# Sum of squares of the first three gate groups on TensorE instead of VectorE, in a gated recurrence followed by a PReLU MLP (one core)

## The chip, the core and the metric

The kernel runs on one core of a Trainium2 chip. The metric is the time of one execution on the device in microseconds (us), here a median over a few runs. The core's engines are TensorE (PE; its weight loads are PEld), VectorE (DVE), ScalarE (ACT), GpSimd (POOL) and SyncE (SP), which here issues all the DMAs. Each engine works through its own instructions in order and waits on semaphores for the others.

## The reference, cut to what matters

```python
# q, k, v, a_re, a_im: (4, 8, 768, 48) f32; w_in (384, 2048), w_out (2048, 384), alpha (2048)
mag = sqrt(a_re*a_re + a_im*a_im)
scale = minimum(mag, 0.999) / (mag + 1e-6)
ar, ai = a_re*scale, a_im*scale                  # complex gate per token and channel
for t in range(768):                             # state S: (4, 8, 48, 48), complex
    S = (ar[t] + i*ai[t])[..., None] * S + outer(k[t], v[t])
    y[t] = q[t] @ real(S)
x = y.transpose(0, 2, 1, 3).reshape(3072, 384)
h = x @ w_in
out = (maximum(h, 0) + alpha * minimum(h, 0)) @ w_out
```

## The kernel before

**Tiling.** The 768 tokens of each of the 4 batches are cut into 6 chunks of 128, so there are 24 *units* (batch, chunk). The gates are made in 9 *groups* (`GATES`): groups 0, 1 and 2 hold 1, 2 and 3 chunks of batch 0, the other six hold 3 chunks each. A group is a tile of 128 partitions by `N` values (3 rows of 128 channels times its tokens: `N` = 384, 768, 1152) in six planes `x, c, f, d, e, y`.

**Gates.** `gates(g, b, c0, c1)` loads `a_re` and `a_im` into `x` and `y` (L255), squares both on ScalarE into `c` and `d` (L265, L267; group 0, which is worked in two halves, L301, L303), adds them on VectorE (L269; group 0 L305), takes roots on ScalarE (L272 to L277; group 0 L310 to L314), corrects with VectorE products that read the sum again (L279 and L289; group 0 L316 and L323), writes unit complex numbers and decays, and then forms running products of the phases (`product`, L416 and L418). The phases of whole chunks leave by the products of L507, the sums of L510 and the DMAs of L512 to a DRAM tile `phs`; the decays leave by L401 to `decs`.

**Units.** `loads` brings each unit's queries and keys (`KQ`, L657, L659), phases (`PP`, L665, read back from `phs`; one buffer) and decays (`T`, L672, read back from `decs`). `unit(u)` rotates queries and keys by the phases (VectorE, L742 and L744, `WQ` and `KQ`), then climbs six levels: at each VectorE multiplies `KQ` by decays (L797, six per unit), ScalarE copies (L820, L836), and TensorE makes 32x32 products into `ps_lv` (`meet`, L759). After the sixth L797 come transposes (L868), state products (L880), level outputs (L900), states (L916 on ScalarE, L918 on VectorE) and L930, which ends `ps_y`. The rows go to DRAM (L949) and come back as `xT` (L962).

**MLP.** `features` (L978, into `ps_h`), PReLU in two steps (ScalarE L985, VectorE L987) and `outputs` (L997, into `ps_o`) for groups of one or two chunks; the last three groups use a form with fewer products (L1097, L1172). The weights come as 64-bit words and are turned to f32 by ScalarE (L588 to L592), GpSimd (L596) and VectorE (L598, L600).

**PSUM.** `ps_h` has two buffers, `ps_o` and `ps_y` one each (`ps_y` spans two banks).

**Order.** Every task is a generator that yields before each step. The string `ORDER` gives the sequence, and with it the order on every engine and in SP's queue of DMAs: one letter runs one step. A to I are the gate groups 0 to 8, J `loads`, K `half_rows`, L `loads_v`, M `pieces`, N and O the weights, P to Z and a to m units 0 to 23, n `loads_x`, o the MLP, p `mixes`, q `late_outputs`. The planning values that the yields carry (`ACT(N, t)` and the like) have no effect when the kernel is built.

Of the kernel before, what the change touches and what calls it, by code (L numbers as in the profile page):

```python
# [9 lines left out]
F32 = mybir.dt.float32  # L10
# [3 lines left out]
AF = mybir.ActivationFunctionType  # L14
ALU = mybir.AluOpType
PSUM = bass.MemoryType.PSUM
DRAM = bass.MemoryType.DRAM

P = 128
# [11 lines left out]
    "AAJMMAABAJAAAAAAAAAAAAAAAAAAAAMMMBJMAAAAAAAAAAKANAOAAAABAAANAAAKANNNABAMAJNBKOAKBOOKAABMAKABAAALOAAB"  # L31
    "LAKNOLNAALBOLANNAALBBLAAKBAKBBAKABABKMAAKBAAOAABAAAAAABABBABAAABAOOABABMANAAAAAAABAAAKBABNABBNBNOBOC"
    "BOCBJNNBLBOJBBOONBBNBBOCBBPBCBPPJLJMJCLKBNBCMBCJBPLBPCBOPPJCPBBBPOBPPBBNBPBBNNBBCPPMLPBLBBPLKBPKBCCC"
    "PLOKBKBPKBBBBCBPKCOOPKBPPPCPBPBCBPPPPBBPBCBBPBBPBBPBPCBPMPBCCBCBPNBKLCCNLCNPCPOCOJDCNDPPPJCOJNNCCCNJ"
    "OCNOOLCNOPCNKOMNNCPQPDJCQDLCDNQPPDQQQLCDQDKQQMCLNDQDOKPQQMODQLOOJQJDKQJDOLCQnOJOLDDJQNJOQLQLOOoLoDDC"
    "QLoQRQoLQQLQooooQQCoQDKNJooooRoMQoQCRCCoooooQoRDQQQCODDCONNCooRQRLoDCLRoMoLoCRRLCoooooCJoRDKCRKooooo"
    "RCDoRQLCDLCoooCoRKoOLCDJCQDCCoLDCRRDDCooooooLCQCooCLCoCoCoLCLCCCLCRCCLCKOCRCRLoCooCRRRCRRoRRCoCRCQQC"
    "CRCQCCoRKCRQRQQCQOORRoRCCQCCooRRCNQDoLoDLoNoDNoooNDoEDNNoEOJoDJRJDRLoooooDDoLDRRRLDRRLRDNDNEJDJSDDRo"
    "oJDESDEDSRDRJESSnJSoLESDoLoLODJSSJDSDLLTSDJoELoooooSSSDLoLooooJSSoDDDoSEDLoooSToSoJooJSSSDoSSDSSoooo"
    "ooSTSDETooooTToSEEoEDoooooSDToSEDTSESSSSDooLDTLoooLEEDSLToLSLoooooDLELoTJDSSSDoooooTTSDSESSSLoDooooo"  # L40
    "SEEDTLLoTKoooooDDDToTEJLDDDDoooooTEUJTDKoDoooKTToDoLoToooTLoUoDJoTLToooToEJoDonooToDEoDTKoUoDJooToUo"
    "EoEUTUEoETEDDDJTooUooDoUUoDooToToTTDoLoLoULoLDULLoooUUoDoLooooDoULoLoELooooLoUULoTLUTLJoooooFUEUoETT"
    "TUUUUTTTUooooTToUETUUFEoUEooooEoUVoUEoooooVVKJJUUEUUEUUoFooLEFLoUoLEUFJVUELoVJoUJooooVJEoFVEJEVoEUoo"
    "oUUUEVoEUoLoVVLEoooEoLEoVEJooooJVEWoFEnVVLoVELoLoooEoKVVEoELVEoJFooooJWoVoVFooWLooLVVEEWoLWVoLWVEFJV"
    "VVJEooVoVoooEKoWKoJEoooVEWWooVWoVoEFWVVVEVVEWELWEELooFEELoWLEoEoLoWWLVLoWEEEEVLLooooooLWEWLEoLEFELEK"
    "FFVVVooWooLooVVVVVFFFVLXKEoEWooooooEWWEEWWJoWWJoooWoEJWoWJoFJWoEWFFWWWWoEoELoLEoJoLoEoFXEooooFooooXo"
    "ooooKXWXLXFWoXoGGXLoXooooJWoLXoLWoFWXoXWFXWoFWXFWWoWXoXFFoFLoXoGFJFnGooooXXoJFoFLoLXXXXLGFLoooooXLFX"
    "XXoGoLFGFLoooooooFXoooGFoJoYJXoJFoJXFGKoooXFYFXoXFYJFooooGXXXYoYXLYFooLXFYFKoLoYoYLXXFZLFXLoXYXFLoXX"
    "XoooYXoFGLGFYYLoYGoFJoYFYJoooFoFZoLFoJoYJGKooooFJGYFYLooYYYLoJYYZGLLFoooooZLoFGYZYZoYZYKJFZZooooYFoZ"
    "YoYFGZYYFYFFYYFZFLFZFFLoYLoooZLooLoFFFFFYFZLFZYYYLFoZLYYFLYoooFZYLaZFLoFoooZZZZoYZZLZoGYFFLLoooZoZGo"  # L50
    "LGoFZJoZFFFGJoooooFooZFFZZFZZZGLoonoFLooLaoFoLoooaJoLoZoaJGoLZooaJaGoaoHoLZZLaaZoHGGoGZGZGGaZLGaLooo"
    "ooaZGaLoaJoZaZaooooGJoHaooHGoooaoaGLaHoooLoGLaaJaHoaJaaJoooooHoGbaoaGHoooaoGaobbJKHoaGaoaoaGaaHoLKoG"
    "JoboLGobLGoLGoooGbLoHGHbLboJbHoGJLaoLbbGLooooGoGHobLGaLaHbLGbabLaabaaGoLaooooLGbboGoGHbGooooJbGbGGKo"
    "bbboJobJbGGbcbbJobGGoooboGcbooooGbGoHbGbGcbbbLGcGLoooGbLcGHcGGJoboJcoLJGGGobLGccLGoobKcbLobHLbobbLoc"
    "obHoGHGdbLGHooooccocGoJoJHoooLcocdJooLconJHLoooocLcHoccccoccLGoJdcGGooocodHocHoHdHoHcGGGcoooGooocGGc"
    "GccccodGLLoooGcodooooLoddJoooLocdoLoIHIoHLdooooLHooLHdcoLdcoLdcLocJHcocddoHoHooKcoooILdocoLHoIHdcdLH"
    "LddoIKdooooJdoIddJoddKdHoHooodoHdoIoHedHHodeHIdddodoHLeHLoLoIHodLHoHLHeIHoLdLoooeeJHeHLoLdddHoooeeoH"
    "JHdedHLoJooooeIoLIeLeoeJddoLHoooLeeoLoHdIHeodJoHIHoooeeoJeeeeoeJeoeIJeoenJHIHoooeJIoeooHeHoHfeeoeHfe"
    "eoLLHoHHJHoHHeHoLfeoLILJHHHHofLooooofeLHfeHfLeHKoeIeLoKffLeHoooooefHeoeLgIIfogJLooooIoooffofoHJILooo"
    "ooHLffoJIoJfHHoooooKHofofJooLfffffofKoJgooHofgIoooggoIHIofofHIoIIoofoHKfooHofogfffoffggoLHLoLogoLoHI"  # L60
    "oLgoooILofnoIfgLgLgLfffoLggJoLgfKoooofooooIgLogfooLfIfofggggggogoohgogIhhLJJJIIhIooooogogoIIoogggggg"
    "oLILogoJIoJgIohJgIILgIgooohLIIgoJgIoIghILhIoIghILoLhhIooooIoIhIoJoLihILJooohhohLoLohLohoooLioJIIoLho"
    "LoJiJooohohooJhhiohhihJhihnoIIIhIoIIhIIIIooohIoIhIioIhihhhhhIihoLihLLLohhhLIIIIIiooooLohhiILiIoLiILo"
    "hLoooiiIoLohihohoLIoooILiIiLoLiiiiiioJioJioIIiIoooioiojoioIiiijIiiJooLojLoJoIoJoLjoooiLoIioLojIjiiiI"
    "jiiooooojjooooLojLiiJoooojLopoLjojiiLoooJjoLoojjJLojLLoooooJojLojooJjjjjjJojjJopjojookkkoojojooojjkj"
    "jojjokLkoLkLokJokoLokLoLoookLjooLjkJkokLLokkLoooLokooooLojjjLokjkjojkjjkojkkLlkookkopkJokJpoookokook"
    "oklkkkkLkLoookJlooLoLolooJokJopoJoLllJklnkLllokoooooklolokooollkkLLLolkoololoooJoLloJoLoooLlmlololoo"
    "oloLoLlooolLmooomololloolpmooolomlomopoomoomomoooomooomoollllllmmomoolomomoooolmoonoolllmmomlmomlmol"
    "lomomoooooooomLooLooooLoLoooLoooooooLoqLoooLooLomLooooLooLooLomLoooooooopooooomoooomoooooooooooooooo"
    "oooooooomomomoomoomomoooomomomoqlmqlmqmmmqqmqoooooqqoqoooooqoqqoqooqoqqooqoqqoqoqooqooqqoooooqoqqoqo"  # L70
    "ooooooooooqoooqoooqqoqqoqooooooooooqqooqoooooqqoqqoqooqoqooqoqqoqqqqqqqqoooooooooooqoqqoqoqooqooqooq"
    "oqoqooqoqoqoooqqqoqqonoooooooooooooooqooqqoqoqqoqqooooooooooooqqoqoqoooqooooooooooooqqqooqooqoooqoqq"
    "oqooooooooqqoooooooooqoooooooooooqooqoooqqoooqoqqqoqooooooooqoqoooqoqooooqqoqqoqooqoqooqqqoqoqqqqqqq"
    "ooooqoooooooqoqqoqooqqqoqoqooooooooooooqqqqqqoqqoooooooooooooooooqqqqoqqoqqooooooooooooooooooqoqqqoq"
    "oqoooooooooooooooooqqooooooooooooqoooqoqoooqoqqoqqoooooooooooqqqooooooqoqqoqqooqoqooqoqqqqqooooooooo"
# [29 lines left out]
def kernel(  # L105
# [32 lines left out]
    nc = tc.nc  # L138
    B, HP, _, D, S = q.shape
    H = 2 * HP  # L140
    DM, DF = w_in.shape
# [19 lines left out]
    ps = ctx.enter_context(tc.tile_pool(name="ps", bufs=1, space=PSUM))  # L161
# [6 lines left out]
    ident = consts.tile([P, P], F32, tag="ident")  # L168
# [22 lines left out]
    for h in (16, 32):  # L191
        by_row[h] = []
        for m in range(HC // h):
            t = next(column)
# [11 lines left out]
    DVE = ACT = POOL = PE = DMA = step  # L206
# [21 lines left out]

    def gates(g, b, c0, c1):
        C = c1 - c0  # L230
        n = C * P
# [26 lines left out]
        if g:  # L258
# [9 lines left out]
            t = yield DVE(N, t)  # L268
            TT(out=c, in0=c, in1=d, op=ALU.add)  # L269

            t = yield ACT(N, t)
            nc.scalar.activation(d, c, AF.Abs_reciprocal_sqrt)  # L272
# [6 lines left out]
            TT(out=e, in0=e, in1=c, op=ALU.mult)  # L279
# [9 lines left out]
            TT(out=c, in0=c, in1=d, op=ALU.mult)  # L289
            ts = yield ACT(N, ts)  # L290
            nc.scalar.activation(c, c, AF.Copy, scale=1.0 / (1.5 * GATE_SCALE))
        else:
            parts = [[z[:, N // 2 * h:N // 2 * (h + 1)] for z in (x, c, f, d, e, y)] for h in range(2)]
            ready, tf, ts, txs = [None, None], [None, None], [None, None], [None, None]

            def enter(h):
                x, c, f, d, e, y = parts[h]
                yield ACT(N // 2, tx)
                nc.scalar.activation(x, x, AF.Identity, scale=1.5, bias=bias_tiny)
                yield ACT(N // 2)  # L300
                nc.scalar.activation(c, x, AF.Square, scale=GATE_SCALE)  # L301
                r = yield ACT(N // 2, t)
                nc.scalar.activation(d, y, AF.Square, scale=1.5 * GATE_SCALE)  # L303
                ready[h] = yield DVE(N // 2, r)
                TT(out=c, in0=c, in1=d, op=ALU.add)  # L305

            def root(h):
                x, c, f, d, e, y = parts[h]
                r = yield ACT(N // 2, ready[h])
                nc.scalar.activation(d, c, AF.Abs_reciprocal_sqrt)  # L310
                r = yield ACT(N // 2)
                nc.scalar.activation(e, d, AF.Square)
                r = yield ACT(N // 2)
                nc.scalar.activation(f, e, AF.Abs_reciprocal_sqrt)  # L314
                yield DVE(N // 2, r)
                TT(out=e, in0=e, in1=c, op=ALU.mult)  # L316
                yield DVE(N // 2)
                STT(out=d, in0=e, scalar=3.0, in1=d, op0=ALU.subtract, op1=ALU.mult)
                for p, w in ((y, -0.75), (x, -0.5)):
                    txs[h] = yield DVE(N // 2)  # L320
                    STT(out=p, in0=p, scalar=w * GATE_SCALE, in1=d, op0=ALU.mult, op1=ALU.mult)
                ts[h] = yield DVE(N // 2)
                TT(out=c, in0=c, in1=d, op=ALU.mult)  # L323
# [937 lines left out]
```

## Time and profile before

| | |
|---|---|
| runs | 816.86, 817.37, 820.89 us; median 817.37 us |
| the profiled execution | 820.38 us, its span 818.6 us, mean granted TensorE clock 0.968 |
| busy, share of the span | TensorE 681.1 us (83%), VectorE 693.9 (85%), ScalarE 520.3 (64%), GpSimd 222.2 (27%) |
| chain that ended last | TensorE 65%, VectorE 14%, DMA 10%, ScalarE 4% |
| DMA | 129.20 MB on SP's queue, 59.3% of 16 engines' span |

The span runs from the first to the last instruction of the profiled execution; what lies around it makes 1.8 us of the execution's own time. A busy share is an average over stages with different limits, so the stretches below matter more than the shares. "L742" is line 742 of the kernel before.

### The profile page before, as it was taken

To read this page: it belongs to the slowest core of one execution; us is meant where nothing else is said; L and a number is where in the kernel's file an instruction comes from. 1 tells how busy PE (TensorE), PEld (TensorE's weight loads), DVE (VectorE), ACT (ScalarE), POOL (GpSimd) and SP (SyncE) were. 2 spreads that over 40 slices of the span, in tenths; PEclk is the share of its full clock that TensorE was granted. 3 is DMA by queue.
4 is the path that set the end of the run, shared out by engine and by line. 5 is a ranking of instruction groups with operands and counts; after the bars stand their busy time and mean duration, and the time that the engine had idled before them with its cause. 6 is when DMAs were issued, how large, how long until landed. Compare 5 with 4: busy or idle time off the path is not lost.

```text
span 818.6 us, 27870 instructions
## 1 busy us (share of the span) xinstructions
PE 681.1 (83%) x11680; PEld 539.0 (66%) x11680; DVE 693.9 (85%) x1191; ACT 520.3 (64%) x1307; POOL 222.2 (27%) x293
## 2 busy tenths in 40 slices
PE   0003128659998999999999999999999999999997
PEld 0003126537776777767777777777777777899997
DVE  5999999999989899999999989998787775456574
ACT  8777998669666777876876697555756544312121
POOL 7231343051604310531245054003200000233342
PEclk9999659979999999999999999999999999999999
DMA  8594895593689589738865867787566622101000
GB/s 242 176 294 128 266 296 158 177 253 101 182 235 197 140 194 272 174 90 279 195 168 141 253 160 180 223 197 184 117 182 134 153 77 56 44 1 40 1 21 20
DMA packets 186598, 130.99 MB, mean 160 GB/s; under 512 B 74728, under 2 KB 176872, under 8 KB 186088
## 3 DMA queue, kind: packets, MB, share of 16 engines
q1 hardware_dynamic: 186472, 129.20, 59.3%
q8 instruction: 92, 1.51, 0.8%
q14 instruction: 34, 0.28, 0.1%
HBM read 100.82 MB, written 35.71 MB: 167 GB/s over the span
## 4 chain that ended last, share of the span: by engine, by line
PE 65%; DVE 14%; DMA 10%; ACT 4%; SPq 2%; issue 2%; POOL 1%; DVEq 0%; ACTq 0%; POOLq 0%
PE ps_o L997 19%; PE ps_h L978 18%; PE ps_m L1172 7%; PE ps_lv L759 5%; PE ps_y L1097 4%; PE ps_h L1097 4%; PE ps_y L900 3%; DVE KQ L797 2%; PE ps_kv L880 2%; PE ps_y L930 2%; DMA VL<-in_v_dram 2%; DVE gate L507 2%; PE ps_kt L868 1%; DVE gate L416 1%; DMA T<-decs 1%
## 5 line engine op out<-in xcount | busy, mean ns | idle before, releaser
L978 PE MATMUL ps_h<-xT,w_in_sb 128*128 128x256 f32 (+1 forms) x960 | 227.0, 369 | 2.1 <-DVE w_in_sb L600 1.6
L997 PE MATMUL ps_o<-w_out_sb,g_sb 128*128 128x384 f32 x576 | 222.1, 501 | 4.8 <-DVE g_sb L987 4.7
L978 PEld LDWEIGHTS ps_h<-xT,w_in_sb 128*128 128x128 f32 x960 | 170.9, 195 | 51.3 <-DVE w_in_sb L600 2.2
L797 DVE TENSOR_TENSOR KQ<-KQ,T 96x1024 f32<-96x1024 f32 x120 | 148.4, 1237 | 25.8 <-PE ps_lv L759 19.2
L997 PEld LDWEIGHTS ps_o<-w_out_sb,g_sb 128*128 128x128 f32 x576 | 102.5, 191 | 44.9 <-DVE g_sb L987 6.5
L985 ACT ACTIVATE g_sb<-ps_h 128x256 f32<-128x256 f32 (+1 forms) x160 | 57.9, 362 | 73.0 <-PE ps_h L978 72.2
L759 PE MATMUL ps_lv<-WQ 96*32 96x32 f32 x2304 | 34.4, 203 | 83.6 <-DVE WQ L742 70.2
L759 PEld LDWEIGHTS ps_lv<-WQ 96*32 96x32 f32 x2304 | 26.3, 116 | 105.9 <-DVE WQ L742 71.0
L916 ACT ACTIVATE St<-St,T 96x48 f32<-96x48 f32 x352 | 84.0, 325 | 4.6 <-DVE St L918 4.3
L987 DVE SCALAR_TENSOR_TENSOR g_sb<-g_sb,al,ps_h 128x256 f32<-128x256 f32 (+1 forms) x160 | 71.3, 446 | 13.7 <-ACT g_sb L985 13.1
L1160 POOL TENSOR_TENSOR sums<-g_sb 128x128 f32<-128x128 f32 x48 | 21.8, 475 | 185.5 <-DMA VL<-in_v_dram 110.6
L416 POOL TENSOR_TENSOR gate<-gate 128x72 f32<-128x72 f32 x42 | 34.5, 822 | 133.7 <-ACT gate L446 130.9
L596 POOL TENSOR_SCALAR top<-top 128x768 f32<-128x768 f32 x16 | 44.1, 2755 | 74.6 <-ACT top L588 63.2
L820 ACT COPY WQ<-KQ 96x1024 f32<-96x1024 f32 x48 | 50.0, 1041 | 18.9 <-DVE KQ L797 18.3
L416 DVE TENSOR_TENSOR gate<-gate 128x576 f32<-128x576 f32 (+5 forms) x84 | 50.7, 604 | 1.1
L900 PE MATMUL ps_y<-A,VL 64*48 64x64 f32 x2304 | 41.9, 220 | 4.4 <-issue 4.3
L900 PEld LDWEIGHTS ps_y<-A,VL 64*48 64x48 f32 x2304 | 39.0, 122 | 6.8 <-issue 6.7
L507 DVE TENSOR_TENSOR gate<-gate 128x1152 f32<-128x1152 f32 (+2 forms) x36 | 42.8, 1220 | 0.8 <-POOL gate L492 0.7
L1135 ACT ACTIVATE rl<-g_sb 128x256 f32<-128x256 f32 x24 | 10.0, 416 | 50.0 <-DVE g_sb L1128 50.0
L773 ACT ACTIVATE A<-ps_lv,columns 128x64 f32<-128x64 f32 x144 | 37.4, 336 | 6.2 <-PE ps_lv L759 5.9
L836 ACT COPY W<-KQ 96x512 f32<-96x512 f32 x48 | 30.8, 641 | 16.2 <-DVE KQ L797 8.7
L759 PE MATMUL ps_lv<-KQ,W 96*32 96x32 f32 x1536 | 24.7, 204 | 18.5 <-ACT W L836 17.4
(168 smaller groups left out, 1355.7 us busy)
## 6 DMA issues: line engine op xcount, KB each, us to landing
T<-decs SPq DMA_DIRECT2D x48, 384.0 KB
PP<-phs SPq DMA_DIRECT2D x24, 387.0 KB
KQ<-in_q_dram SPq DMA_DIRECT2D x48, 192.0 KB
decs<-gate SPq DMA_DIRECT2D x7, 1152.0 KB
phs<-gate SPq DMA_DIRECT2D x14, 576.0 KB
KQ<-in_k_dram SPq DMA_DIRECT2D x40, 192.0 KB
vsc<-in_v_dram SPq DMA_DIRECT2D x48, 144.0 KB
VL<-vsc SPq DMA_DIRECT2D x48, 144.0 KB
```

The lines of the kernel that those rows point to most:

```text
L416: on(4 * k).tensor_tensor(out=m, in0=w[:, 1::-1].unsqueeze(2).to_broadcast([P, 2, 2, k]), in1=pairs_of(u), op=ALU.mult)
L507: TT(out=m[:, a], in0=U5[:, 1 + a], in1=turned(off3, o)[:, a].unsqueeze(1).unsqueeze(3).to_broadcast([P, L // 2, nb, 2]), op=ALU.mult)
L759: nc.tensor.matmul(t[64 * i + j:64 * i + j + HC // 2, p], lhsT=keys(n, g), rhs=queries(n, g), start=True, stop=True)
L797: nc.vector.tensor_tensor(out=x, in0=x if x0 is None else x0, in1=m, op=ALU.mult)
L900: nc.tensor.matmul(o, lhsT=Vp[h][64 * i:64 * i + 64, s, e_ * D:(e_ + 1) * D], rhs=a, start=False, stop=False)
L916: nc.scalar.activation(St[:, n], before[:, n], AF.Copy, scale=T[0:D2, n, TL - 4 + s:TL - 3 + s])
L978: nc.tensor.matmul(p, lhsT=w_in_sb[:, f // 2, kk, f % 2 * P:(f % 2 + 1) * P], rhs=x_of[m][:, kk], start=(kk == 0), stop=(kk == NK - 1))
L985: nc.scalar.activation(gt, p, AF.Relu, scale=-1.0)
L987: nc.vector.scalar_tensor_tensor(out=gt, in0=gt, scalar=al_1[:, f:f + 1], in1=p, op0=ALU.mult, op1=ALU.add)
L997: nc.tensor.matmul(sums[0], lhsT=gt[:, c * P:(c + 1) * P], rhs=w_out_sb[:, f], start=(f == 0), stop=(f == NF - 1))
L1097: nc.tensor.matmul(o, lhsT=lhs, rhs=rhs, start=(at in (0, 5)), stop=(at in (4, 8)))
L1172: nc.tensor.matmul(banks[k][:, half], lhsT=lhs, rhs=rhs, start=(j == 0 and half == 0), stop=(j == NF // 2 - 1 and at in (2, 3, 5, 6)))
```

## The change

In groups 0, 1 and 2 the addition of the two squares on VectorE (L269 and L305) is gone. TensorE multiplies each of the two planes by the identity and sums both products in PSUM: two matmuls for each bank. Group 0 takes a buffer of `ps_h` for each half (192 columns), group 1 the two banks of `ps_y` (384 columns each), group 2 both buffers of `ps_h` and `ps_o` (384 columns each). The steps that read the sum now read PSUM: one ScalarE root and two VectorE products for each piece. Group 2's piece is a bank, so each of these three steps becomes three instructions. Groups 3 to 8 are as before. The string `ORDER` is another one.

```diff
+SUMMED = 3
...
+    def bank_views(banks, n):
+        if banks == ["y"]:
+            z = ps.tile([P, 2, 512], F32, tag="y", name="ps_y")[:, :, 0:n // 2]
+            return [(z, lambda row: row.rearrange("p (z s) -> p z s", z=2))]
+        n //= len(banks)
+        return [(ps.tile([P, DM], F32, tag=tag, name="ps_" + tag, bufs=2 if tag == "h" else 1)[:, 0:n],
+                 lambda row, i=i: row[:, n * i:n * (i + 1)]) for i, tag in enumerate(banks)]
+
+    def sum_of_squares(z, a, b_):
+        for i in range(z.shape[1] if len(z.shape) > 2 else 1):
+            parts_ = [x[:, i] if len(z.shape) > 2 else x for x in (z, a, b_)]
+            for j in range(2):
+                nc.tensor.matmul(parts_[0], lhsT=ident, rhs=parts_[1 + j], start=j == 0, stop=j == 1)
...
-            t = yield DVE(N, t)
-            TT(out=c, in0=c, in1=d, op=ALU.add)
+            if g < SUMMED:
+                banks = {1: ["y"], 2: ["h", "h", "o"]}[g]
+                t = yield PE(4 * N * 1.68e-3, t, takes=[R[z] for z in banks])
+                sums_ = bank_views(banks, N)
+                for z, row in sums_:
+                    sum_of_squares(z, row(c), row(d))
+            else:
+                t = yield DVE(N, t)
+                TT(out=c, in0=c, in1=d, op=ALU.add)
+                sums_ = [(c, lambda row: row)]
...
-            nc.scalar.activation(d, c, AF.Abs_reciprocal_sqrt)
+            for z, row in sums_:
+                nc.scalar.activation(row(d), z, AF.Abs_reciprocal_sqrt)
...
-            TT(out=e, in0=e, in1=c, op=ALU.mult)
+            for z, row in sums_:
+                TT(out=row(e), in0=row(e), in1=z, op=ALU.mult)
...
-            TT(out=c, in0=c, in1=d, op=ALU.mult)
+            for z, row in sums_:
+                TT(out=row(c), in0=z, in1=row(d), op=ALU.mult)
...
-                ready[h] = yield DVE(N // 2, r)
-                TT(out=c, in0=c, in1=d, op=ALU.add)
+                ready[h] = yield PE(2 * N * 1.68e-3, r, takes=(R["h"],))
+                square[h] = bank_views(["h"], N // 2)[0][0]
+                sum_of_squares(square[h], c, d)
...
-                nc.scalar.activation(d, c, AF.Abs_reciprocal_sqrt)
+                nc.scalar.activation(d, square[h], AF.Abs_reciprocal_sqrt)
...
-                TT(out=e, in0=e, in1=c, op=ALU.mult)
+                TT(out=e, in0=e, in1=square[h], op=ALU.mult)
...
-                TT(out=c, in0=c, in1=d, op=ALU.mult)
+                TT(out=c, in0=square[h], in1=d, op=ALU.mult)
```

The last part of the change replaces the whole of `ORDER`, the string of letters. In the new string the number of steps of each task is the same, but nearly every stretch of it differs; what that moves on each engine is read from the built programs.

## Prediction

> **What bounds the kernel now.** The page's slices come first, because the busy shares (DVE 85%, PE 83%) hide that two engines take turns.
>
> ```profile
> PE   0003128659998999999999999999999999999997
> ...
> DVE  5999999999989899999999989998787775456574
> ...
> PEclk9999659979999999999999999999999999999999
> ```
>
> The same by stretches (start:end, length, then busy us of PE, PEld, DVE, ACT, POOL, the granted clock, DMA share, GB/s):
>
> ```profile
> 0.00:20.00 20.00, 0.00 (x0) 0.00 (x0) 11.24 (x40) 16.07 (x32) 14.37 (x31) 1.00 0.86 239
> 40.00:60.00 20.00, 0.66 (x32) 0.53 (x32) 18.58 (x35) 12.93 (x16) 6.63 (x3) 1.00 1.06 289
> 100.00:120.00 20.00, 3.74 (x192) 3.07 (x192) 19.97 (x23) 18.73 (x20) 5.43 (x2) 0.50 1.10 330
> 220.00:240.00 20.00, 20.00 (x304) 15.60 (x303) 19.36 (x27) 12.84 (x40) 2.13 (x1) 1.00 0.65 193
> 500.00:600.00 100.00, 100.00 (x1911) 74.78 (x1911) 87.60 (x120) 60.02 (x182) 20.95 (x32) 1.00 0.71 177
> ```
>
> From 20 to about 235 us VectorE is full and TensorE has gaps; then TensorE is full to the end. So time is won where VectorE reaches the point of handover sooner, or where less TensorE work stands behind it. I take unit 5's sixth L797 as that point (it ends at 236.3 us): there VectorE's work so far plus TensorE's work still to come is largest, 221.9 + 565.3 = 787.2 us. The missing 31.4 us of the span are 14.4 us in which VectorE was idle before the point (8.8 of them in the first 20 us) and about 17 us of TensorE waits and tail behind it.
>
> The chain of waits shows the one transfer that VectorE meets head on in that stage, phases written and read back (start, length):
>
> ```profile
> 40.44 4.53 DMA phs<-gate
> ...
> 45.98 6.69 DMA PP<-phs
> ...
> 86.26 4.23 DMA phs<-gate
> ...
> 97.73 9.52 DMA KQ<-in_k_dram
> ```
>
> In the timeline unit 0's first product waits for it; the bracket is idle time before the instruction and what ended it:
>
> ```profile
> 52.87 1.22 DVE L742 TENSOR_TENSOR WQ<-KQ,PP 96x1024 f32<-96x1024 f32 x1 [1.07 <-DMA PP<-phs]
> ```
>
> **VectorE, the work itself.** Rows by shape (busy us and mean ns behind the bar):
>
> ```profile
> L782 DVE TENSOR_TENSOR A<-ps_lv,mask 128x512 f32<-128x512 f32 x48 | 32.7, 680 | 0.0
> L269 DVE TENSOR_TENSOR gate<-gate 128x1152 f32<-128x1152 f32 x7 | 9.6, 1366 | 0.0
> L507 DVE TENSOR_TENSOR gate<-gate 128x768 f32<-128x768 f32 x4 | 3.6, 950 | 0.0
> L507 DVE TENSOR_TENSOR gate<-gate 128x384 f32<-128x384 f32 x4 | 2.0, 552 | 0.0
> L305 DVE TENSOR_TENSOR gate<-gate 128x192 f32<-128x192 f32 x2 | 0.7, 359 | 4.3 <-ACT gate L303 4.3
> ```
>
> Instructions that follow closely overlap by some 0.08 us, so I count steps in the timeline: 2 x 0.36 (L305), 0.87 (768 wide) and 1.27 (1152 wide) go, 2.86 us. Group 2's two products become three of 384 each, 3 x 0.47 = 1.41 for 1.27, twice: +0.28. Net -2.6 us. An operand in PSUM I count at nothing: L782 reads one, and its 680 ns lie on the line through 552 and 950 ns of the SBUF rows (685 at 512 wide). [...]
>
> ScalarE reads the sum at L272 and L310. A 384-wide copy from PSUM takes 0.48 us (L870), so three cost at most 3 x 0.48 - 1.17 = 0.3 us more; ScalarE is idle for 7 us of 40 to 60, which hides it.
>
> **TensorE, the work itself.** 14 matmuls come: 4 of 192 columns, 4 and 6 of 384. L997 is 384 wide and in the chain two of them take 1.29 us at full clock; at half clock one takes 1.28 in a row of them, 1.49 alone. So the three groups take 1.3, 2.6 and 3.9 us, or double. All lie before 60 us, where TensorE does 0.66 us of work. They cost nothing by themselves; their latency is on the gate chains.
>
> Group 0 is a chain from the first load. The sum takes 0.36 us now; with half clock and the first matmul starting on the first square, the root starts at about 5.9 us, not 5.56, and the second half's at 7.2, not 6.6. Against that the new order moves six reductions (0.63 us, L195) out of this chain to its front. VectorE reaches L380 at 13.2 us in both. So the 0.7 us that group 0 saves is not gained: +0.7 against the work sum. Group 1's sum takes 5.2 us at half clock, but its squares move up to about 15 us, and VectorE reaches the product behind it at 24.1, when the roots are ready at about 23.8: no wait, with 0.3 to spare.
>
> **The order.** The built programs hold the same other instructions in another sequence. I add up for both, with the mean step of each shape in this trace, VectorE's work up to unit 5's sixth L797 and TensorE's work behind the transposes that follow: 221.9 + 565.3 before, 217.9 + 565.3 after. TensorE's part is the same. So VectorE has 4.0 us less to do there: 2.6 by the change, 1.4 moved behind. At units 3, 4 and 6 the same sum falls by 2.2, 2.9 and 3.3. SP's queue hardly moves: at each unit's `PP` the bytes issued before it differ by under 1 MB up to unit 11.
>
> But idle time moves too. Unit 0: `phs` leaves VectorE 1.5 us earlier, `PP` lands at about 51.2, VectorE arrives at 51.3: the 1.07 us wait goes. Unit 1: the new order puts its L742 only 8.8 us of VectorE work behind group 1's last L510; now it is 12.9 us of time. The round trip needs 4.2 (write) + 0.4 (issue) + 6.7 (read, from unit 0) = 11.3 us. VectorE then stands 2.5 us at L742, with the rest of its queue behind it. If the read takes 5.4 us as the `T<-decs` piece at 115 us did, 1.2; if 9.5 as the `KQ` piece above, 5.4.
>
> Sum at the handover: -4.0 + 0.7 - 1.1 + 2.5 = -1.9 us, between -3.2 and +1.0 by the read's time. TensorE runs full from there and carries it to the end. From the profiled execution's own 820.4 us that is 818.5; that run lies 3.0 above the median of 817.37, so the forecast is 815.5.
>
> **Rivals.**
> *More is gained.* The read is early and the smaller waits close: without the wait at unit 1 the sum is -4.4, 813.0. VectorE's idle time grows from 14.4 to 21.2 us between units 5 and 7, mostly by waits for `T` and TensorE; if the new order saves half of that, 3.4, it is -7.8, 809.6. For it: the two-engine sum falls at nearly every unit. Against: those are waits for DMA and TensorE, not work.
> *Slower: first products run ahead of their phases.* The new order shortens VectorE's work between a group's last L510 and the first L742 that needs its phases: for group 1 from 11.9 to 8.8 us, for group 3 (unit 6) from 11.2 to 9.6. Below the round trip each missing us is a standing VectorE. With the 9.5 us read the first costs 5.4 and the second, at 14.1 - 9.6, 4.5: -4.0 + 0.7 - 1.1 + 9.9 = +5.5, 822.9. It decides from 4.4 us of such waits. Against: at unit 6 VectorE already waits 3.3 us for `T`, which would cover most of the second.
> *The sums hold up TensorE's queue.* Group 2's six matmuls stand ahead of unit 0's first L759. They can start at about 50.3 us (squares), or 54.5 if ScalarE is no earlier than now, and take 7.7 at half clock: they end between 58 and 61 and the two L759 blocks (0.66 each) behind them between 59.3 and 62.3, when VectorE wants the second L797 at about 58.4. Price 0.9 to 3.9 us: 816.4 to 819.4. The trace shows the clock rising while TensorE works: matmuls from 120.1 us are slow until 123.7. [...]
>
> **Chances.** Forecast 0.42, more gained 0.28, products ahead 0.20, queue 0.10. About 0.5% (4.1 us) is what a measurement of this kernel can tell from no change. Faster by more: 0.26 of the second case and 0.03 of the first. Slower by more: 0.16 of the third, and 0.04 where it and the queue's come together, 0.20. Within: 0.51. The range takes the first case whole, most of the second and most of the third: 809.5 to 822.0.
>
> **What would show it.** Right: VectorE idle 2 to 3 us before unit 1's first product with `PP<-phs` as the releaser; none before unit 0's; unit 5's sixth decay product ending near 234.4 instead of 236.3; the products on PSUM at 0.35, 0.95 and 0.55 us; TensorE as full as now behind it. Wrong: roots waiting long for the sums in group 1, the first `ps_lv` block after 58 us, the point at 236 or later, or TensorE waits after 240 us that are more than a few us off the present ones.

## The result, and the profile after

The changed kernel takes 831.08 us (median of 4 runs, 828.65 to 832.09) against 819.13 us for the kernel before (median of 4, 816.86 to 821.63): a ratio of 1.0141, 95% interval 1.0097 to 1.0184. It is slower by 12 us; 815.5 had been forecast, and 822.0 was the top of the range. The profiled execution took 832.09 us, its span is 830.1 us, the mean granted clock 0.92 instead of 0.968. Lines in the units' code and the MLP are 33 further down than before (L742 is now L775, L797 is L830, L987 is L1020); the sums' matmuls are L244.

The page's slices of TensorE, VectorE and the clock:

```profile
PE   2033229639998989999999999999999999999997
...
DVE  4999999989978989899999998998888666556564
...
PEclk7555558869999999999999999999999999999999
```

TensorE now works in the first slices, and VectorE dips to 7 and 8 in more slices of the first half than before. By stretches (columns as in the prediction):

```profile
0.00:20.00 20.00, 5.34 (x12) 3.94 (x13) 9.38 (x38) 14.28 (x31) 11.63 (x30) 0.77 0.82 235
40.00:60.00 20.00, 7.37 (x44) 3.91 (x44) 19.45 (x34) 13.36 (x16) 7.09 (x3) 0.53 0.99 281
220.00:240.00 20.00, 20.00 (x438) 15.19 (x439) 19.38 (x25) 11.57 (x36) 6.86 (x4) 1.00 0.52 154
240.00:260.00 20.00, 17.33 (x246) 13.36 (x234) 14.26 (x24) 11.72 (x32) 0.00 (x0) 0.91 0.94 240
300.00:320.00 20.00, 18.81 (x371) 13.75 (x371) 17.84 (x22) 14.88 (x43) 0.56 (x3) 0.91 0.57 143
```

The kernel before in the last two of these stretches:

```profile
240.00:260.00 20.00, 17.74 (x343) 13.66 (x342) 16.20 (x24) 13.18 (x29) 5.31 (x10) 1.00 0.96 217
300.00:320.00 20.00, 19.89 (x290) 14.57 (x289) 19.31 (x29) 15.37 (x36) 1.85 (x3) 1.00 0.93 276
```

The sums are seen in 0 to 20 us and 40 to 60 us, nearly all of them slow: group 0's products took 544 ns each, where 192 columns at a granted clock of 1.00 take 326 (`ps_m`, L1205); group 1's (17.55 to 22.20 us) and group 2's (52.63 to 59.80 us) stand, but for their last ones, at a granted clock of 0.50 (10.99 to 21.23 and 24.64 to 58.78 us). TensorE is full from 220 to 240 us as before. Behind that both kernels have gaps and the changed one has more: 17.33 against 17.74 and 18.81 against 19.89 of 20 us, at a clock of 0.91 in both stretches where the kernel before has 1.00.

VectorE's work fell as worked out: 693.9 us busy before, 691.1 after. Its idle time did the opposite. Adding up VectorE's idle time along the trace, up to the end of the sixth decay product of each unit:

| unit | before: end (idle so far) | after: end (idle so far) |
|---|---|---|
| 0 | 75.2 (11.7) | 75.0 (14.1) |
| 3 | 189.3 (14.1) | 193.8 (20.7) |
| 5 | 236.4 (14.4) | 241.5 (22.6) |
| 6 | 266.4 (19.0) | 275.2 (29.7) |
| 8 | 317.0 (22.1) | 327.4 (35.0) |
| 23 | 684.8 (63.7) | 698.5 (82.2) |

So 5 us are lost by the point of handover and another 5 by unit 8 (10.4 us); from there on little is added (13.7 us at unit 23, where VectorE is no longer the bound, and 11.5 us at the end of the span). The timeline of VectorE shows the waits (in brackets the idle time and what ended it), first the weights, which ScalarE and GpSimd turn to f32 and which come later than before:

```profile
19.02 0.56 DVE L631 TENSOR_SCALAR top<-top 128x768 uint32<-128x768 uint32 x1 [1.23 <-POOL top L629]
...
21.00 0.96 DVE L633 CUSTOM_DVE_ANT_0 w_in_sb<-top,w_in_sb 128x1536 uint16<-128x1536 uint16 x1 [0.87 <-ACT w_in_sb L625]
```

and later unit 6's first product and a PReLU step:

```profile
248.71 1.22 DVE L775 TENSOR_TENSOR WQ<-KQ,PP 96x1024 f32<-96x1024 f32 x1 [3.71 <-DMA ysc<-T]
...
300.54 0.48 DVE L1020 SCALAR_TENSOR_TENSOR g_sb<-g_sb,al,ps_h 128x256 f32<-128x256 f32 x1 [3.31 <-ACT g_sb L1018]
```

The table of TensorE's waits from 236 us on (line, what it waited for, total us, times, longest), first before, then after:

```profile
PE ps_y L900 <- issue: 3.9, 4, 1.3
PE ps_y L930 <- DVE St L918: 1.2, 1, 1.2
PE ps_lv L759 <- ACT W L836: 1.1, 1, 1.1
```

```profile
PE ps_y L963 <- DVE St L951: 2.7, 1, 2.7
PE ps_h L1011 <- DVE g_sb L1020: 2.0, 1, 2.0
PE ps_y L933 <- issue: 1.6, 1, 1.6
```

The two largest both stand behind VectorE: the wait for St's sum has grown from 1.2 to 2.7 us, and the one of 2.0 us is new. After each the granted clock is one half for 3.4 us (253.34 to 256.75 and 301.12 to 304.54 us; the 0.91 above: 3.4 of 20 us at half).

**An account that closes.** Split the span at the end of unit 5's sixth decay product. From the part behind it take TensorE's idle time and half of the time at half clock (six `ps_h` records take 2.56 us there and 1.29 at full clock, in e6's chain; the last 5 us left out). What remains is TensorE's work, and it is the same in every kernel of this study, whatever its order (574 to 577 us):

| kernel | point | behind it | TensorE idle | at half clock | what remains |
|---|---|---|---|---|---|
| before | 236.4 | 582.3 | 7.1 | 0 | 575.2 |
| changed | 241.5 | 588.6 | 9.0 | 6.8 | 576.2 |
| e1 | 241.0 | 607.6 | 23.2 | 17.1 | 575.9 |
| e5 | 237.7 | 586.6 | 7.0 | 6.8 | 576.2 |
| e6 | 238.9 | 603.5 | 21.8 | 13.7 | 574.9 |
| e7 | 244.7 | 586.9 | 6.4 | 10.2 | 575.3 |
| e16 | 239.1 | 586.1 | 7.9 | 3.4 | 576.5 |

The changed kernel's 11.5 us of span are 5.1 to the point, 1.9 of TensorE's idle time, 3.4 of half clock and 1.0 that stays open. Single executions scatter by some us (e9's profiled one took 836.1 us, its median is 827.8), so verdicts below go by the medians and the traces say where.

### The profile page after: what moved, and what is told of

The parts are those of the page before. It is cut to its first block, busy times and chain, and to the rows that moved or that the text cites. A ratio compares the mean times of both kernels' runs of the same rounds, so it can differ in the third digit from the quotient of the medians.

```text
span 830.1 us, 27894 instructions
## 1 busy us (share of the span) xinstructions
PE 702.2 (85%) x11708; PEld 549.7 (66%) x11708; DVE 691.1 (83%) x1191; ACT 518.9 (63%) x1309; POOL 214.8 (26%) x293
## 3 DMA queue, kind: packets, MB, share of 16 engines
q1 hardware_dynamic: 186472, 129.20, 58.4%
q8 instruction: 92, 1.51, 0.8%
## 4 chain that ended last, share of the span: by engine, by line
PE 65%; DVE 13%; DMA 7%; ACT 6%; SPq 5%; issue 3%; POOL 2%; DVEq 0%; ACTq 0%; POOLq 0%
PE ps_o L1030 19%; PE ps_h L1011 18%; PE ps_m L1205 6%; PE ps_lv L792 5%; PE ps_y L1130 4%; PE ps_h L1130 4%; DMA KQ<-in_q_dram 3%; PE ps_y L933 3%; DVE KQ L830 3%; PE ps_kv L913 2%; PE ps_y L963 2%; PE ps_kt L901 2%; DVE gate L540 1%; SPq L737 1%; SPq L690 1%
## 5 line engine op out<-in xcount | busy, mean ns | idle before, releaser
L1030 PE MATMUL ps_o<-w_out_sb,g_sb 128*128 128x384 f32 x576 | 225.4, 507 | 2.3 <-DVE g_sb L1020 2.0
L1011 PEld LDWEIGHTS ps_h<-xT,w_in_sb 128*128 128x128 f32 x960 | 173.0, 196 | 59.6 <-DMA xT<-ysc 6.1
L830 DVE TENSOR_TENSOR KQ<-KQ,T 96x1024 f32<-96x1024 f32 x120 | 149.0, 1241 | 19.0 <-PE ps_lv L792 12.9
L1018 ACT ACTIVATE g_sb<-ps_h 128x256 f32<-128x256 f32 (+1 forms) x160 | 57.5, 360 | 81.5 <-PE ps_h L1011 80.9
L1020 DVE SCALAR_TENSOR_TENSOR g_sb<-g_sb,al,ps_h 128x256 f32<-128x256 f32 (+1 forms) x160 | 71.2, 445 | 27.3 <-ACT g_sb L1018 27.0
L449 POOL TENSOR_TENSOR gate<-gate 128x72 f32<-128x72 f32 x42 | 29.4, 701 | 143.6 <-ACT gate L479 140.8
L977 ACT COPY T<-ps_y 48x256 f32<-48x256 f32 x96 | 32.3, 364 | 13.5 <-PE ps_y L963 12.8
```

The costliest lines, as they stand in the source:

```text
L449: on(4 * k).tensor_tensor(out=m, in0=w[:, 1::-1].unsqueeze(2).to_broadcast([P, 2, 2, k]), in1=pairs_of(u), op=ALU.mult)
L830: nc.vector.tensor_tensor(out=x, in0=x if x0 is None else x0, in1=m, op=ALU.mult)
L1011: nc.tensor.matmul(p, lhsT=w_in_sb[:, f // 2, kk, f % 2 * P:(f % 2 + 1) * P], rhs=x_of[m][:, kk], start=(kk == 0), stop=(kk == NK - 1))
L1018: nc.scalar.activation(gt, p, AF.Relu, scale=-1.0)
L1020: nc.vector.scalar_tensor_tensor(out=gt, in0=gt, scalar=al_1[:, f:f + 1], in1=p, op0=ALU.mult, op1=ALU.add)
L1030: nc.tensor.matmul(sums[0], lhsT=gt[:, c * P:(c + 1) * P], rhs=w_out_sb[:, f], start=(f == 0), stop=(f == NF - 1))
```

## The experiments

### The two halves of the change (e1 to e4)

The letters of `ORDER` stand for the same steps in both kernels, so the strings can be exchanged and also spliced: the first n letters of the one, then all steps that are left in the sequence of the other.

```diff
 e1: SUMMED = 3
-ORDER = <the new string>
+ORDER = <the string of the kernel before>
 e2: the kernel before
-ORDER = <its string>
+ORDER = <the new string>
 e3: sums; first 480 letters of the new string, the rest in the old sequence
 e4: sums; first 480 letters of the old string, the rest in the new sequence
```

> The sums of groups 0 to 2 on TensorE as in the changed kernel, but the ORDER string of the kernel before. Theory 'the order': the new order, not the sums, makes the 12 us; then the sums bring VectorE about 2 us less work (2.6 off, some of it lost at the start of group 0) and the kernel comes out at 0.994 to 1.002 of before, 814 to 821 us. Rival 'the sums': waiting for TensorE at half clock and the held PSUM banks make it; then 1.010 to 1.018 here too, 827 to 834 us. Rival 'both by halves': 1.004 to 1.008.

> The other half of the change alone: the kernel before, sums on VectorE, with the new ORDER string. Theory 'the order': as slow as the changed kernel or up to 3 us slower, 1.013 to 1.020 of before (830 to 835 us), and VectorE's idle time up to unit 5's sixth decay product at 20 us or more instead of 14. Rival 'the sums': 0.997 to 1.002, 816 to 821 us. Rival 'they fit only together': the order was found for the sums and is worse without them, 1.02 or more.

> Sums on TensorE; the first 480 letters of the new ORDER (to about 75 us, unit 0's last products), then all steps that are left in the old order. It tells where in the order the cost lies. Theory 'start': the weights' loads behind the queries' loads in SP's queue, and the waits they make at 19 to 25 us, cost and are carried to the end: 1.005 or more of before (823 us or more). Theory 'later': the waits at units 3 to 8 (T, vsc, xT behind others in SP's queue, 175 to 300 us) make it: 0.995 to 1.003, 815 to 822 us.

> Sums on TensorE; the first 480 letters of the old ORDER, then all steps that are left in the new order. Theory 'start': 0.995 to 1.003 of before, 815 to 822 us. Theory 'later': 1.008 to 1.016, 826 to 832 us.

Measured against 825.09 us of the kernel before on that chip: e1 850.09 us, 1.0305 (1.0274 to 1.0335); e2 848.79, 1.0294 (1.0260 to 1.0328); e3 847.17, 1.0268 (1.0237 to 1.0300); e4 836.26, 1.0126 (1.0101 to 1.0151). Neither "the order" nor "the sums" had foreseen that either half alone loses twice as much as both together; only the rival "they fit only together" of e2 had (1.02 or more). e3 falls into the range of "start" and e4 into that of "later", which cannot both be the place. e3 is the strangest: up to unit 4 VectorE is where it is in the kernel before (211.9 against 211.3 us), the letters behind are the old ones, and yet 22 us go. TensorE's waits in e1 tell where:

```profile
PE ps_lv L792 <- issue: 10.8, 6, 3.9
PE ps_y L933 <- issue: 8.0, 3, 3.3
PE ps_o L1030 <- issue: 2.5, 1, 2.5
PE ps_y L963 <- issue: 1.1, 1, 1.1
```

"issue" means that TensorE waited for nothing that the profile shows. That is 22.4 us in 11 waits; the kernel before has 3.9. Counting TensorE's records in the trace one by one, the instruction behind each such wait of over 0.3 us is the 193rd or 194th of a run of 256, in all six traces that I had by then. The page gives the size of what could be waited for:

```profile
q8 instruction: 92, 1.51, 0.8%
```

92 packets of 1.51 MB are 16.4 KB each, and TensorE's 23,640 records in the kernel before make 92.3 runs of 256. In that kernel's trace the six waits on "issue" of over 0.3 us from 133 us on stand at records 1729, 2497, 9153, 9921, 14529 and 19137, counted from 0, and the distances between them are all multiples of 256. So I read from the traces that TensorE's instructions arrive in blocks of 256. In e1 the packet next to each wait starts 2.2 to 2.8 us before TensorE goes on (in the kernel before 2.3 to 3.0 us). About 80 of the 92 blocks in e1 end without such a wait, and the rest cost up to 3.9 us each. The sums add 56 records (14 f32 matmuls, two passes of a weight load and a product each) ahead of the units. That shifts every block end behind them.

### Block ends, moved on purpose (e5 to e8)

The test adds instructions that do nothing where TensorE has nothing else to do (they take 0.84 us from 1.65 us on in e6 and 2.67 us from 22.3 us on in e5):

```diff
+            if g == 1:
+                pad_ = ps.tile([P, 8], F32, tag="misc", name="ps_pad")
+                for _ in range(28):          # e5: 101, e8: 99
+                    nc.tensor.matmul(pad_[0:2, 0:2], lhsT=ident.bitcast(BF16)[:, 0:2],
+                                     rhs=ident.bitcast(BF16)[:, 0:2], start=True, stop=True)
```

e6 and e7 have 28 of them (56 instructions, as many as the sums add), in the kernel before and in e2. e5 and e8 have 101 and 99 in e3 and e1, which with the sums' 56 and a few waits make 256 within one, so that block ends fall where they fall in the kernel before.

> As e3 (sums on TensorE, 480 letters of the new order, then the old), and 101 matmuls of 2 columns more on idle TensorE behind group 1's sums: 202 instructions, so that every later TensorE instruction stands at the same place modulo 256 as in the kernel before. Nobody reads their result. Theory 'blocks': TensorE's instructions come in blocks of 256 (the 16 KB packets of q8), and the waits for nothing that the trace of e3 shows (12 of them, about 22 us, each near the 193rd record of a block, 6.8 us of half clock behind them) arise where a block's end falls among short matmuls; the 56 instructions of the sums moved all ends. Then they go: 0.993 to 1.002 of before, 815 to 827 us on this chip. Rival 'misfit': an order serves only the program it was found for; then 1.022 to 1.030 as e3.

> The kernel before with nothing changed but 28 matmuls of 2 columns (56 instructions, as many as the sums add) on TensorE behind the addition of group 1, when TensorE has nothing to do; nobody reads them. Theory 'blocks': 1.015 to 1.035, with waits for nothing on TensorE that sum to 15 us or more, at the same instructions as in e1 and e3. Rival 'misfit': 0.998 to 1.003, since neither the order nor the work of any full engine changes.

> As e2 (adds on VectorE, the new order) and 28 such matmuls, so that TensorE's blocks end where they do in the changed kernel. Theory 'blocks': TensorE's waits for nothing fall from 12.7 us to under 4, and what is left is what the new order alone costs: 1.010 to 1.018 of before (the changed kernel has 1.014). Rival 'misfit': 1.026 to 1.033 as e2. If the new order costs nothing by itself: 0.997 to 1.004.

> As e1 (sums on TensorE, the whole old order) and 99 such matmuls: blocks end as in the kernel before. Theory 'blocks': the 22 us of waits for nothing and 8.5 us of half clock go; what stays is the sums' latency in an order not made for them (VectorE's idle time up to unit 0's sixth decay product 18.5 us instead of 11.7) less 2.6 us of work: 1.001 to 1.007. Rival 'misfit': 1.027 or more.

Measured against 824.88 us: e5 824.04 us, 0.9985 (0.9963 to 1.0008); e6 845.33, 1.0249 (1.0212 to 1.0286); e7 837.24, 1.0139 (1.0105 to 1.0172); e8 829.64, 1.0059 (1.0031 to 1.0086). All four fall into the ranges of "blocks", and "misfit" is out. e6 is the plainest: 28 products that nobody reads, on an idle engine, make the kernel 2.5% slower. Its chain of waits (start, length, what; lines 5 further down than in the kernel before):

```profile
278.09 0.61 PE ps_lv L764 x45
278.70 2.59 issue
281.29 0.42 PE ps_lv L764 x10
281.71 2.86 PE ps_o L1002 x4
```

and the stretches around it:

```profile
270.00:278.00 8.00, 8.00 (x190) 6.45 (x190) 7.71 (x20) 6.18 (x20) 0.00 (x0) 1.00 0.84 215
278.00:281.00 3.00, 0.70 (x59) 0.57 (x54) 0.13 (x1) 1.50 (x4) 1.21 (x3) 0.95 0.42 81
281.00:287.00 6.00, 5.71 (x21) 3.90 (x22) 3.58 (x4) 1.05 (x1) 0.97 (x2) 0.50 0.31 66
```

In a run of 32-column products TensorE stands for 2.59 us. Then the clock is 0.50, and four `ps_o` products take 2.86 us, which take 1.29 us at full clock elsewhere in the same chain. The wait goes with blocks that TensorE runs through quickly, such as those of short products. Over all traces, behind the point, TensorE waited over 0.3 us on "issue" at every one of the 19 block ends whose 252 records before had taken under 2.2 us, at 24 of 31 from 2.2 to 3.4 us, at 18 of 62 from 3.4 to 4.2 us, at 26 of 307 from 4.2 to 6 us and at 2 of 884 above. A fit of the wait's size, 3.6 us less that time, is rough: single waits lie 2 us and more off it. By it both `ORDER` strings sit at a shift of block ends that costs under 1 us, and the median of all shifts would cost some 10 us. That is an estimate from the two kernels' own traces; of other shifts, runs have only those of e1, e2, e3 and e6, with 12.7 to 22.4 us of such waits behind the point. Each string did better at the shift of TensorE's instructions that it was found with (the old one 1.0305 in e1 and 1.0059 in e8, the new one 1.0294 in e2 and 1.0139 in e7), and that had looked like "they fit only together".

With block ends put right, the halves can be read. Old order and sums: +0.6% (e8). New order and adds: +1.4% (e7), which is the changed kernel's own 1.0141. New order for 480 letters and sums, then the old: no change (e5). So the sums gain nothing that can be measured, and the loss comes with the new order's letters behind 480. The waits on "issue" are not equal in these kernels, though: behind the point the profiled executions have 4.2 us (e5), 2.0 us (e7) and 7.2 us (e8) against 3.9 before, so some 3 us of e8's 4.8 can be theirs. e8 shows what the new order is good for; VectorE's timeline in e8 (lines 5 further down):

```profile
27.83 0.18 DVE L454 TENSOR_TENSOR gate<-gate 128x24 f32<-128x24 f32 x1 [4.05 <-ACT gate L484]
...
67.23 1.22 DVE L835 TENSOR_TENSOR KQ<-KQ,T 96x1024 f32<-96x1024 f32 x1 [2.87 <-PE ps_lv L797]
```

In the old order the roots of group 1 come late behind the sums, and the copies that VectorE waits for stand behind them on ScalarE (4.05 us). Unit 0's decay product waits 2.87 us for `ps_lv`, and that wait comes through ScalarE too:

```profile
64.16 0.49 ACT L303 ACTIVATE gate<-ps_o 128x384 f32<-128x384 f32 x1 [1.03 <-PE ps_o L244]
...
65.75 0.63 ACT L874 COPY W<-KQ 96x512 f32<-96x512 f32 x1
...
66.44 0.66 PE L797 MATMUL ps_lv<-KQ,W 96*32 96x32 f32 x32 [1.92 <-ACT W L874]
```

Group 2's roots wait for the sums (the last of three is shown), ScalarE's copy stands behind them, and the second `ps_lv` block waits 1.92 us for the copy, with TensorE idle. Waits of these two lengths are not in the changed kernel: the first is 0.45 us there, the second is gone.

### Where in the new order (e9 to e12)

```diff
 e9, e10: e5 with 850 and 1250 letters of the new order instead of 480 (101 and 98 products of padding)
 e11: e5, e12: the changed kernel, each with
-    "AABBMJAAAAAAMAAAJAAJAAJAAAAAABAAAAAAAAAMMMAAAAAAAKNAAMBA...
+    "AABBMAAAAAAMAAAAAAAAAAAAABAAAAAAAAAMMMAAAAAAAKNAAMJJJJBA...
```

> As e5, but the new order holds for 850 letters (to about unit 3, 190 us) before the old takes over; 101 matmuls of padding put TensorE's blocks behind the change of order where the kernel before has them. e5 (480 letters) had 0.9985. Theory 'middle': the waits of VectorE between units 1 and 3 (weights' upper halves at 118 us, T at 175, group 3's roots at 180) make the loss of the new order: 1.003 to 1.010. Theory 'late': the loss is made where TensorE takes over (units 5 to 8): 0.996 to 1.002 here.

> As e9 with 1250 letters of the new order (to about unit 6, 260 us), 98 matmuls of padding. Theory 'late': now the handover is the new order's, with its first product of unit 6 that waits for phases, the wait of TensorE behind it and the half clock: 1.005 to 1.014. Theory 'middle': no more than e9 has.

> As e5, and the four steps that issue unit 0's queries and keys come behind the first weights in SP's queue (as they nearly do in the old order). In e5 VectorE waits 1.9 us between 18 and 25 us for weights that are turned to f32, and the loads of queries and keys stand ahead of them. Theory: these waits go, unit 0's first product stays where it is or comes up to 2 us earlier, and the gain is carried to the end: 0.994 to 0.998. Rival: the 1.9 us come back at the next wait: as e5, 0.997 to 1.000.

> The changed kernel with the same four steps behind the first weights, nothing else. If the new order's later part sets the end by waits of its own, 2 us won at the start are lost there: 1.012 to 1.016 as the changed kernel (e4, whose unit 0 is 5.6 us later than the changed kernel's, ended no later). If the start is carried: 1.009 to 1.012.

Measured against 825.42 us: e9 827.83 us, 1.0031 (0.9996 to 1.0065); e10 828.26, 1.0046 (1.0010 to 1.0082); e11 824.74, 0.9993 (0.9961 to 1.0025); e12 831.15, 1.0079 (1.0044 to 1.0115). The loss grows with the letters, 0.9985, 1.0031, 1.0046 and about 1.01 for the whole string; no one place holds it, and the steps between neighbours are within the intervals. e9 lies at the lower edge of "middle" and e10 just under the range of "late", so these runs do not tell the two apart; besides, the profiled executions of e9 and e10 have 8.1 and 6.2 us of waits on "issue" behind the point, e5 4.2. In e11 the waits for weights did go (VectorE's idle time at unit 0 falls from 13.4 to 11.6 us, the point from 237.7 to 236.1), but the time did not fall: its median lies in the rival's range, and the test is inconclusive, since 1.9 us is less than the interval. e12 lies below both of its ranges. It is lower than the changed kernel's ratio on other chips, as a start that is carried on would have it, with intervals that overlap.

### Mending the waits (e13 to e16)

Two waits of the changed kernel can be followed to what they stand behind. The first is on SP's queue; the timeline of SP in the changed kernel:

```profile
234.82 0.56 SPq L545 DMA_DIRECT2D phs<-gate  x1
235.43 4.03 SPq L737 DMA_DIRECT2D VL<-in_v_dram  x5
239.56 0.38 SPq L545 DMA_DIRECT2D phs<-gate  x1
...
244.55 0.32 SPq L698 DMA_DIRECT2D PP<-phs  x1
```

Five loads of values stand 4.03 us between the two writes of group 3's phases. The read of `PP` must wait for the second; it leaves at 244.55, and VectorE stands until 248.71 with St's sum (L951) behind it, for which TensorE waits 2.7 us. The bracket above names another DMA that landed last; that it is the phases is read from the order of the issues, and e14, which moves them, bears it out. But this wait is not the new order's alone. In the kernel before, five loads stand at the same place, and VectorE waits there too:

```profile
228.74 3.25 SPq L704 DMA_DIRECT2D VL<-in_v_dram  x5
232.09 0.54 SPq L512 DMA_DIRECT2D phs<-gate  x1
...
242.26 1.22 DVE L742 TENSOR_TENSOR WQ<-KQ,PP 96x1024 f32<-96x1024 f32 x1 [2.80 <-issue]
```

From the last sum of phases to this product it takes 13.9 us before and 14.1 us after, so of the 3.71 us only 0.9 are new. The second wait is ScalarE's:

```profile
292.30 3.72 POOL L521 TENSOR_TENSOR gate<-gate 128x144 f32<-128x144 f32 x1 [2.23 <-ACT gate L519]
```

```profile
298.32 0.32 ACT L527 ACTIVATE gate<-gate 128x144 f32<-128x144 f32 x1 [3.90 <-POOL gate L525]
...
300.13 0.38 ACT L1018 ACTIVATE g_sb<-ps_h 128x256 f32<-128x256 f32 x1
```

L527 of group 4 waits 3.90 us for GpSimd with the PReLU step L1018 behind it in ScalarE's queue; VectorE's L1020 waits for that (3.31 us above), and TensorE for L1020 (2.0 us). The edits move letters only:

```diff
 e14: letters 1150 to 1199 of the changed kernel's ORDER
-DDoLoLTDLLoooooUDoLUDLooooLTTToLUUTLTUKToTLoooooUJ
+DDooTDoooooUDoUDLLLLLJLooooLTTToLUUTLTUKToTLoooooU
 e15: e14 and letters 1516 to 1548
-oFFVELoEFFWJWFWJoWWJWJooooooWFoJE
+oFFVELoFFWJWFWJoWWJWJooooooEWFoJE
 e16: e15 and the first letters of e12
```

> The changed kernel itself, on the chip of the next three, as their measure: 1.010 to 1.018 of before. Above all three of them if the waits named there are the cause; equal to them if not.

> The changed kernel with six letters moved in ORDER: five loads of values of unit 5 stand behind the second write of group 3's phases in SP's queue instead of ahead of it, and the read of unit 6's phases follows at once (both are DMAs on SP's queue, no engine's work moves). Theory 'waits': the phases land 3 to 4 us earlier, VectorE's 3.7 us at unit 6's first product go, TensorE's 2.7 us behind it and the half clock after it (1.7 us) with them: 3 to 4.5 us less than e13, 0.004 to 0.006 of before. Rival 'many small waits': the time comes back at the next wait for T or values; as e13 within 0.002.

> As e14, and one step of group 4 (ScalarE's copy L527, which waits 3.9 us for GpSimd at 294 us with the PReLU behind it) stands 20 letters later, behind the next PReLU steps. Theory 'waits': VectorE's 3.3 us at L1020, TensorE's 2.0 us and 1.7 us of half clock go too: 6 to 8 us less than e13, 0.007 to 0.010 of before; TensorE's idle time behind the handover 3 to 5 us instead of 9. Rival 'many small waits': within 0.003 of e13.

> As e15, with unit 0's loads of queries and keys behind the first weights as in e12: all three places of the new order mended. Theory 'waits': 8 to 10 us less than e13, 0.998 to 1.005 of before. If it is 1.010 or more, the cause is none of the three.

Measured against 823.50 us: e13 (the changed kernel) 831.64 us, 1.0108 (1.0072 to 1.0145); e14 831.64, 1.0101 (1.0066 to 1.0137); e15 829.29, 1.0073 (1.0042 to 1.0103); e16 827.01, 1.0050 (1.0023 to 1.0077). e14 is a miss for "waits": the wait for phases falls to 1.11 us, and the next one takes its place, since the state's start was behind the same loads:

```profile
245.35 1.22 DVE L775 TENSOR_TENSOR WQ<-KQ,PP 96x1024 f32<-96x1024 f32 x1 [1.11 <-DMA VL<-in_v_dram]
...
256.82 0.55 DVE L838 TENSOR_TENSOR St<-St,start 96x384 f32<-96x384 f32 x1 [3.00 <-DMA St<-in_v_dram]
```

e15 and e16 bring 2.4 and 4.6 us by the medians, a third and a half of what was expected, and less than their own waits' sum. Only e16's gain over e13 is clear of the noise (2.1 to 7.6 us when the single runs are resampled). TensorE's idle time behind the point stayed at 8.9 us in e15, where 3 to 5 had been expected. TensorE's waits in e16:

```profile
PE ps_o L1030 <- DVE g_sb L1020: 3.1, 1, 3.1
PE ps_y L933 <- issue: 2.2, 3, 1.2
PE ps_kt L901 <- ACT T L904: 1.5, 1, 1.5
```

The wait at unit 6 is still 3.1 us, at another instruction. So the three places together are a part of the loss (4.6 of 8.1 us, e13 to e16), and the rest returns at the next wait of the same stretch. What makes the remaining half per cent is open: e16's expectation of 0.998 to 1.005 was met only at its upper end. No kernel of this study beats the kernel before by more than its interval; e5 comes nearest.

## Why the prediction was wrong

- **The bound and the handover** were right. The point moved and everything behind it with it, and TensorE's work behind it is the same (575.2 and 576.2 us in the account).
- **VectorE's work** was right: -2.6 forecast, -2.8 measured in all. An operand in PSUM costs nothing that shows here:

```profile
L306 DVE TENSOR_TENSOR gate<-gate,ps_h 128x384 f32<-128x384 f32 x2 | 1.0, 550 | 0.0
L306 DVE TENSOR_TENSOR gate<-gate,ps_y 128x768 f32<-128x768 f32 x1 | 1.0, 955 | 0.0
...
L348 DVE TENSOR_TENSOR gate<-gate,ps_h 128x192 f32<-128x192 f32 x2 | 0.7, 346 | 4.9 <-ACT gate L346 4.9
```

  550, 955 and 346 ns stand against 552, 950 and 359 ns from SBUF.
- **The sums on TensorE** took about what was said (4.65 us for group 1's, 5.2 forecast; VectorE reaches L413, before L380, at 13.1 us as before; group 1's first root starts at 23.65 us, 23.8 forecast). "They cost nothing by themselves" missed that 56 more instructions shift all block ends. In the changed kernel the new string hides that (2.9 us of such waits behind the point, 3.9 before); with the old string (e1) it is the largest price, 22.4 us of them.
- **The order's work**: -4.0 us forecast up to the point, -3.1 measured (222.0 to 218.9).
- **Idle time** is the step that failed. I let it grow from 14.4 to 16.5 us by pricing the waits for `PP` at units 0 and 1 alone; it is 22.6. Unit 0's 1.07 us did go. Unit 1's 2.5 us did not come: its product starts at 96.1 us, 9.7 us behind the last sum of phases, without a wait, so the round trip is shorter than the 11.3 us I took. What came were waits that I had not looked for: weights behind the loads of `KQ` (1.23 and 0.87; e11 moved the loads, and these two went), later weights at 118 us (1.42), `T` at 175 us (1.14), a later group's squares at 180 us (1.03; the expectation of e9 calls them roots). "SP's queue hardly moves" compared bytes ahead of each `PP`, and not which DMA stands ahead of which.
- **"TensorE runs full from there and carries it to the end"** failed too: 1.9 us more of idle time and 3.4 us by half clock, priced at nothing.
- **The slower rival** had one of its two places right. At unit 6 the round trip is the 14.1 us that it took, though of other parts (it had a 9.5 us read; here five loads stand between the writes), which is luck. VectorE waits 3.7 us there, near its 4.5, but 2.8 of them are in the kernel before, and what the wait sets off on TensorE (2.7 us and half clock) was not in it. The argument against it misread the trace: 3.3 us is the sum of three waits for `T` in the whole execution, of which unit 6 has 1.34, and the largest part of the some 7 us of idle time between units 5 and 7 is the 2.80 us at unit 6's first product, not `T` or TensorE.
- **The queue rival**'s sign was there (the first `ps_lv` block at 59.7 us instead of 54.1) without a wait of VectorE behind it, and that is luck: VectorE was itself 3 us later there than forecast (the second decay product at 61.54 us, 58.4 forecast). Its upper price was added wrongly: 54.5 + 7.7 is 62.2 and not 61, so it reached 5.1 us and not 3.9. In the old order the late sums do make VectorE wait, through ScalarE (e8).

Together: 234.4 us was forecast for the point, 241.5 came (+7.1), and behind it 588.6 instead of 582.3 (+6.3).

## What to carry to other kernels

An order that was searched for on the chip is fitted to things that no engine's work shows, so a small change has to be judged with the whole string rebuilt, and one half of such a change says little by itself. Before you blame an order or an operation, look for waits on "issue" and count at which instruction they fall: a few idle instructions ahead tell within one run whether block ends are the cause (28 idle products made 1.0249 of the kernel before in e6). And price a new order by the queue: for each wait that is moved, what stands behind it on the same engine, because the waits that are taken away came back here at the next instruction in line (in e14 3.71 us fell to 1.11, and 3.00 us stood at the next).

## What the hardware did that I had not expected

- TensorE can stand at the same place of every 256 records with nothing on another engine to wait for: 0.3 us (the changed kernel) to 3.9 us (e1) at a time, 4 times in the kernel before and 11 times in e1 behind the point. That a block of instructions is run through before the next one has come is my reading; it fits most of these waits, and no trace shows it directly.
- The clock fell after waits from 1.42 us on. In all traces, of TensorE's waits between 245 and 700 us, none of the 28 from 1.0 to 1.41 us was followed by half clock, 13 of 32 from 1.42 to 1.98 us were, and 25 of 34 from 2.0 us on, for 3.4 us or twice that (in the changed kernel from 253.34 to 256.75 us, behind a wait of 2.67 us).
